# A second chunk's second product by Strassen, with the sums of w_out made one chunk earlier

## The chip, the cores and the metric

The kernel runs on one core of a Trainium2 chip. The metric is the device time of one execution in microseconds. TensorE (PE) multiplies matrices, VectorE (DVE) and ScalarE (ACT) work element by element, GpSimd (POOL) casts values and issues transfers, and SyncE (SP) issues transfers. Each engine takes its own instructions in order; semaphores tie them together.

## The reference

```python
# attention: 8 batches, 8 heads, 576 positions, head size 64
scores = q @ k.T / 8
# heads 0-3: a causal window of 32; heads 4-7: a causal window of 128, every 4th position
attn   = softmax(where(mask, scores, -1e9)) @ v
x      = attn with heads side by side      # 4608 tokens x 512
# feed-forward
h   = x @ w_in                             # 512 x 2048
g   = relu(h) ** 2
out = g @ w_out                            # 2048 x 512, float32
```

## The kernel before

The 4608 tokens are cut into nine chunks of 512 for the feed-forward part; attention runs over eight batches of 576 tokens. Products are in fp16 with sums in float32.

**First product** (`mm1_gen`). For each of 16 slices of 128 hidden features (`ffc`), four matmuls of 512 columns fill one PSUM bank `ph`; ScalarE writes relu into `rt` (L328), VectorE squares it into `g` (L329). A slice is two steps of a generator.

**Second product.** There are three forms. Chunk 0 goes by `mm2_by_rows_gen`, which takes w_out in the order of its four pieces `wo0` to `wo3` as they are loaded. Chunk 1 goes by `mm2_gen`, 64 matmuls of 512 columns (L450), two to a step, 32 steps; ScalarE copies each bank `po` into `ot` (L471) and SP stores it, four stores of 256 KB. Chunks 2 to 8 go by `mm2_strassen_gen`: the matrix of 512 tokens x 2048 features times 2048 x 512 is cut into quarters, and seven products of half size take the place of eight. Each product is 16 matmuls of 256 columns (L382), four to a step, 28 steps in all; the results are gathered in three banks `pa`, `pb` and `pc`. This form needs sums of the quarters of g and of w_out:

- of g, per chunk: `sum_of_g` (L338, L339), called after slices 11 and 15, two instructions each; the difference at L413 before the first product; the difference at L425 after the fourth. They read and write `gs0`, `gs1` and `g`.
- of w_out, once: `sums_of_w_out`, eight differences (L355) into `wt0` to `wt3`. They are handed out one at a time, after each even slice of chunk 1's first product.
- the results: three ScalarE copies (L398) and three VectorE additions (L409), two stores of 512 KB.

**Order.** The order is written out by hand. Attention is emitted piece by piece, and after each piece `pump(n)` emits n steps of the pending feed-forward generator, so TensorE has matmuls while ScalarE takes exponentials and VectorE multiplies by masks (`AT`, L572 and L573) and divides (`rcp`, `xs`, `xd`, L614 and L619). Chunk 0's second product is mixed with batch 1's attention, chunk 1 with batch 2's, chunk 2 with batch 3's. For batch 2 the pump is called with 22, then four times 4, then ten times 2. Attention's PSUM tiles (`ps`, `pz`, `pav`, `paw`) take turns in two double banks.

**Transfers around it.** Batch 3's q and k of the sliding heads are loaded by POOL into `ns`, reordered by VectorE into `nr` (L120), written by SP to device memory as `dp` (L224) and read back by a transposing transfer into `QKTp` (L232), which batch 3's first scores `ps` (L582) read. `turn_and_load` emits this chain, with the loads of the next v (`sv`, `sd`) between the write and the transposes; for batch 2 it is called after the third `av_sliding`. The dilated heads go from device memory to device memory (`dd`, POOL, L214) and by transposes into `QKTd` (L236). w_out's pieces are loaded by POOL (L153): pieces 0 and 1, then batch 1's q and k, then piece 2, and piece 3 later. SP's queue is in order, so stores that stand behind transposes wait for their issue.

## Time and profile before

| | |
|---|---|
| median of 8 executions | 306.73 us (304.44 to 309.36) |
| the profiled execution | 309.36 us, span 307.4 us |
| TensorE busy | 288.0 us, 94% |
| VectorE busy | 212.2 us, 69% |
| ScalarE busy | 173.3 us, 56% |
| POOL busy | 63.5 us, 21% |
| matmuls of 512 columns, second product (L450) | 128, 33.1 us busy |
| sums of w_out (L355) | 8, at 66.4 to 79.5 us |

The profile is one execution, here the slowest of the eight; its span runs from the first to the last instruction, and about 2 us of the time lie outside it. Times inside it are counted from the span's start. A busy matmul overlaps the next one, so TensorE's rate is read from the distance of starts or from the chain, not from the mean of one.

### The profile page before, as it was taken

What the parts mean: (1) busy time and instruction counts of PE and PEld (TensorE: products, weight loads), DVE (VectorE), ACT (ScalarE), POOL (GpSimd) and SP (SyncE); (2) the same over time, 40 slices, a digit from 0 to 9 for tenths busy, and PEclk for the clock granted to TensorE, in tenths of its full rate; (3) what the DMA queues carried; (4) which work ended last, traced back from release to release, by engine and by line L of the source; (5) the groups of instructions that cost most, each with busy time, mean ns of one, the idle gap of its engine ahead of it and who ended that gap; (6) DMA issues with size and microseconds to landing.
All of it is one profiled execution on the core that took longest, in us unless ns stands there. A gap on an engine that the chain in (4) does not pass through costs nothing.

```text
span 307.4 us, 6893 instructions
## 1 busy us (share of the span) xinstructions
PE 288.0 (94%) x2762; PEld 193.3 (63%) x2762; DVE 212.2 (69%) x437; ACT 173.3 (56%) x293; POOL 63.5 (21%) x112
## 2 busy tenths in 40 slices
PE   0978999899999899999999999999999999999994
PEld 0635554455555458855898988557855875785583
DVE  7685447858961589579947994899489934834652
ACT  1764647677844683386439633964396346425620
POOL 4292007201340630530026102700230000000000
PEclk9999999999999999999999999999999999999998
DMA  7699996999969999996799989998992230003004
GB/s 110 139 179 215 206 208 95 177 220 232 146 120 226 227 203 205 175 262 121 147 140 276 182 151 178 282 174 172 158 263 25 44 115 34 2 1 139 0 1 136
DMA packets 77471, 46.77 MB, mean 152 GB/s; under 512 B 58432, under 2 KB 69184, under 8 KB 77440
## 3 DMA queue, kind: packets, MB, share of 16 engines
q1 hardware_dynamic: 68688, 32.71, 50.1%
q0 software_dynamic: 8752, 13.63, 26.5%
q8 instruction: 21, 0.34, 0.5%
q14 instruction: 10, 0.08, 0.1%
HBM read 36.70 MB, written 16.52 MB: 173 GB/s over the span
## 4 chain that ended last, share of the span: by engine, by line
PE 72%; DVE 13%; DMA 7%; ACT 3%; issue 2%; POOL 1%; SPq 0%; DVEq 0%; POOLq 0%
PE ph L305 30%; PE pa L382 14%; PE po L450 8%; PE pb L382 7%; DVE AT L573 4%; DMA QKTp<-dp 4%; PE pc L382 3%; DVE g L329 3%; DMA vd<-vd 2%; PE paw L647 2%; DMA ns<-in_q_dram 2%; PE ps L582 2%; DVE xd L619 2%; PE pf L516 1%; ACT AT L572 1%
## 5 line engine op out<-in xcount | busy, mean ns | idle before, releaser
L305 PE MATMUL ph<-xT,wi 128*128 128x512 f16 (+1 forms) x640 | 134.2, 359 | 0.7 <-ACT xT L684 0.7
L328 ACT ACTIVATE rt<-ph 128x512 f16<-128x512 f32 x144 | 86.3, 609 | 44.6 <-PE ph L305 41.5
L305 PEld LDWEIGHTS <-wi 128*128 128x128 f16 x640 | 68.2, 114 | 45.9 <-issue 0.6
L329 DVE TENSOR_TENSOR g<-rt 128x512 f16<-128x512 f16 x144 | 62.5, 445 | 38.5 <-ACT rt L328 37.4
L382 PEld LDWEIGHTS <-g 128*128 128x128 f16 x448 | 43.3, 98 | 6.2
L382 PEld LDWEIGHTS <-gs 128*128 128x128 f16 x336 | 32.0, 98 | 5.3 <-DVE gs L339 1.7
L450 PE MATMUL po<-wo,g 128*128 128x512 f16 x128 | 33.1, 379 | 0.0
L409 DVE TENSOR_TENSOR ov<-pb,ov 128x512 f32<-128x512 f32 x14 | 9.7, 692 | 27.3 <-PE pb L382 13.9
L382 PE MATMUL pa<-wt,gs 128*128 128x256 f16 x224 | 27.6, 273 | 0.8 <-DVE gs L339 0.8
L382 PE MATMUL pb<-wt,g 128*128 128x256 f16 x224 | 27.1, 273 | 0.0
L169 POOL CAST vp<-sv 128x512 f16<-128x512 f32 x24 | 15.1, 660 | 57.3 <-DMA sv<-in_v_dram 57.3
L398 ACT COPY ov<-pa 128x512 f32<-128x512 f32 x14 | 8.2, 587 | 31.8 <-PE pa L382 31.8
L177 POOL CAST vd<-sd 128x512 f16<-128x512 f32 (+1 forms) x32 | 21.8, 707 | 10.8 <-DMA sd<-in_v_dram 10.2
L619 DVE TENSOR_TENSOR xd<-paw,rcp_d 80x512 f16<-80x512 f32 (+1 forms) x32 | 21.9, 684 | 1.1
L573 DVE TENSOR_TENSOR AT<-AT,maskd 128x576 f16<-128x576 f16 x32 | 20.2, 667 | 1.3 <-ACT AT L572 0.4
L572 ACT ACTIVATE AT<-ps 128x576 f16<-128x576 f32 x32 | 19.2, 658 | 2.7 <-PE ps L582 2.3
L572 ACT ACTIVATE AT<-pz 128x576 f16<-128x576 f32 x32 | 19.7, 694 | 1.4 <-PE pz L601 1.2
L573 DVE TENSOR_TENSOR AT<-AT,maskp 128x576 f16<-128x576 f16 x32 | 15.5, 493 | 6.4 <-ACT AT L572 4.8
L619 DVE TENSOR_TENSOR xs<-pav,rcp_p 96x512 f16<-96x512 f32 x24 | 16.5, 686 | 0.8
L398 ACT COPY ou<-pa 128x512 f32<-128x512 f32 x14 | 8.2, 587 | 15.0 <-PE pa L382 15.0
L450 PEld LDWEIGHTS <-g 128*128 128x128 f16 x128 | 10.4, 97 | 8.3
L647 PEld LDWEIGHTS <-AT 128*128 128x128 f16 x256 | 12.0, 98 | 5.6 <-PE paw L647 1.3
(81 smaller groups left out, 278.1 us busy)
## 6 DMA issues: line engine op xcount, KB each, us to landing
sv<-in_v_dram SPq DMA_DIRECT2D x14, 288.0 KB, 5.4
dp<-nr SPq DMA_DIRECT2D x12, 288.0 KB, 3.9
out_dram<-ou SPq DMA_DIRECT2D x6, 512.0 KB, 4.1
out_dram<-ov SPq DMA_DIRECT2D x6, 512.0 KB, 4.4
sd<-in_v_dram SPq DMA_DIRECT2D x8, 320.0 KB, 5.7
ns<-in_k_dram POOLq DMA_DIRECT2D x8, 288.0 KB, 6.9
ns<-in_q_dram POOLq DMA_DIRECT2D x8, 288.0 KB, 7.9
sd<-in_v_dram SPq DMA_DIRECT2D x8, 256.0 KB, 5.5
```

Of the source, the lines that this page charges most:

```text
L169: nc.gpsimd.tensor_copy(vp[b % 2][:, m : m + 2, :, 0:D], sv[:, :, m : m + 2, :].rearrange("p h m d -> p m h d"))
L177: nc.gpsimd.tensor_copy(vd[b % 2][p0:P, t, c : c + 2, :, 0:D], sd[p0:P, t, :, D * c : D * (c + 2)].rearrange("p h (c d) -> p c h d", d=D),)
L305: nc.tensor.matmul(ph[:, t0:t1], wi4[ffc // 4][:, dmk, :, ffc % 4], xT[:, dmk, x0 : x0 + t1 - t0], start=(dmk == 0 and t0 == 0), stop=(dmk ...
L328: nc.scalar.activation(rt, ph[:], ACTF.Relu)
L329: nc.vector.tensor_mul(g[:, ffc, :], rt, rt)
L382: nc.tensor.matmul(banks[bank][:, t], a(k, t), b(k), start=(new and t == 0 and k == 0), stop=(k == HF - 1), skip_group_check=True,)
L398: nc.scalar.copy(ot, banks[A])
L450: nc.tensor.matmul(po, g[:, ffc, t * P : (t + 1) * P], wo[ffc // 4][:, ffc % 4, :], start=(ffc == 0), stop=(ffc == NFF - 1),)
L572: nc.scalar.activation(AT[:, u, 0:UW], ps[:, :, 0 : UW // 2], ACTF.Exp, scale=scale)
L573: nc.vector.tensor_mul(AT[:, u, 0:UW], AT[:, u, 0:UW], mask)
L619: nc.vector.tensor_tensor(out=x, in0=pv, in1=rb, op=ALU.mult)
L647: nc.tensor.matmul(pav[:, e, h * (D + 2) : h * (D + 2) + D + 1], AT[:, 4 + h, off : off + P], vd[b % 2][:, t, 2 * a + e, h, 0 : D + 1], st ...
```

## The change

Chunk 1 also uses `mm2_strassen_gen`, so `mm2_gen` and its stores go. `mm1_gen` no longer hands out w_out's sums, and calls `sum_of_g` for chunk 1. The eight sums of w_out are emitted in another order, first the four that read pieces 0 and 2, then the four that read pieces 1 and 3. The first four are emitted one by one after each of the four transposing steps of batch 1's q and k, the other four together after batch 1's `attn_values`.

```diff
@@ mm1_gen
             nc.vector.tensor_mul(g[:, ffc, :], rt, rt)
-            if c == 1 and ffc % 2 == 0:
-                next(w_sums)
             if sums and ffc % 4 == 3 and ffc >= HF:
                 sum_of_g(g, ffc - 3, ffc + 1)
@@ sums_of_w_out
-        def w(r, c):
-            return [wo[2 * r + n][:, :, HM * c : HM * (c + 1)] for n in range(2)]
-
-        def t(k):
-            return [wt[k][:, 4 * n : 4 * (n + 1)] for n in range(2)]
-
-        for k, x, y in (
-            (0, w(0, 1), w(0, 0)),
-            (1, w(1, 1), t(0)),
-            (2, w(1, 1), w(0, 1)),
-            (3, w(1, 0), t(1)),
-        ):
-            for o, a, b in zip(t(k), x, y):
+        def w(r, c, n):
+            return wo[2 * r + n][:, :, HM * c : HM * (c + 1)]
+
+        for n in range(2):
+            t = [wt[k][:, 4 * n : 4 * (n + 1)] for k in range(4)]
+            for o, a, b in (
+                (t[0], w(0, 1, n), w(0, 0, n)),
+                (t[1], w(1, 1, n), t[0]),
+                (t[2], w(1, 1, n), w(0, 1, n)),
+                (t[3], w(1, 0, n), t[1]),
+            ):
                 nc.vector.tensor_sub(o, a, b)
                 yield
 
     w_sums = sums_of_w_out()
+
+    def sum_w_out(n):
+        for _ in range(n):
+            next(w_sums)
@@ store
-        if c:
-            nc.sync.dma_start(out=out[(c * 4 + t) * P : (c * 4 + t + 1) * P, :], in_=ot)
-        elif t % 2:
+        if t % 2:
             first_out.append((t - 1, halves[c]))
             if t == 1:
                 leave_first()
-
-    def mm2_gen(c, g):
...
@@ moe_gen
         g = hidden(c)
-        yield from mm1_gen(c, g, c > 1)
-        yield from (mm2_strassen_gen if c > 1 else mm2_gen)(c, g)
+        yield from mm1_gen(c, g, True)
+        yield from mm2_strassen_gen(c, g)
@@ batch 1's attention
     for hp in range(2):
         t_sliding(1, n, hp, True)
         pump(3)
+        sum_w_out(1)
     for a in range(2):
         t_dilated(1, m, a, True)
         pump(2)
+        sum_w_out(1)
     attn_scores(1, 2, 1)
     dp = []
     attn_values(1, 1, True, lambda: dp.append(keep_sliding_qk(2, by_token(2, ns))))
+    sum_w_out(4)
     pump(1000)
```

## Prediction

> **What bounds the kernel now.** I read the page first (busy shares), then the chain of work that ended last, then VectorE's timeline and the waits around the stretch that the change touches.

> ```profile
> PE 288.0 (94%) x2762; PEld 193.3 (63%) x2762; DVE 212.2 (69%) x437; ACT 173.3 (56%) x293; POOL 63.5 (21%) x112
> ...
> PE 72%; DVE 13%; DMA 7%; ACT 3%; issue 2%; POOL 1%; SPq 0%; DVEq 0%; POOLq 0%
> ```

> TensorE is the bound over the whole span, but 13% of the chain is VectorE and 7% DMA, so what a saved matmul is worth depends on where it sits. The chain at its undisturbed end gives the price of both forms of the second product:

> ```profile
> 251.30 13.81 PE ph L305 x64
> 265.12 1.75 PE pa L382 x16
> 266.86 0.87 PE pc L382 x8
> ```

> 64 matmuls of 512 columns take 13.81 us (216 ns each); 16 of 256 columns take 1.75 us (109 ns each). Next, the chain where chunk 1 ends and batch 3's attention begins:

> ```profile
> 94.68 2.69 PE po L450 x12
> 97.37 0.88 PE ph L305 x4
> ...
> 98.62 5.36 DMA QKTp<-dp
> ...
> 104.02 0.43 PE ps L582 x12
> ```

> Chunk 1's last 12 matmuls run to 97.37, chunk 2's first 24 to 102.55, and then TensorE stands until 104.02 for batch 3's transposed q and k:

> ```profile
> PE ps L582 <- DMA QKTp<-dp: 1.5, 1, 1.5
> ```

> So whatever chunk 1 saves is handed to a TensorE that already waits 1.5 us for a transfer. What starts that transfer is VectorE's copy `nr`:

> ```profile
> 79.49 1.10 DVE L355 TENSOR_TENSOR wt<-wo,wt 128x1024 f16<-128x1024 f16 x1
> 80.51 1.64 DVE L573 TENSOR_TENSOR AT<-AT,maskd 128x576 f16<-128x576 f16 x2
> 82.07 0.41 DVE L329 TENSOR_TENSOR g<-rt 128x512 f16<-128x512 f16 x1
> 82.41 0.81 DVE L573 TENSOR_TENSOR AT<-AT,maskd 128x576 f16<-128x576 f16 x2
> 83.19 0.20 DVE L614 RECIPROCAL rcp_p<-pav 96x8 f32<-96x8 f32 x1
> 83.42 0.69 DVE L619 TENSOR_TENSOR xs<-pav,rcp_p 96x512 f16<-96x512 f32 x1
> ...
> 86.50 0.80 DVE L120 COPY nr<-ns 128x2304 f16<-128x2304 f16 x1
> ```

> From 75.07 to 84.1 VectorE has no gap; `nr` is queued at the end of that run. After it come, on SP's queue, the writes of `dp` (87.33), the loads of v, and the transposes (95.68).

> **The change part by part.** *TensorE.* 64 x 216 ns = 13.8 us go, 7 products x 16 x 109 ns = 12.2 us come: -1.6 us. Weight loads (98 ns) still fit under a 109 ns matmul. [...] The trace has 216 and 109 ns for just such pairs, so I take -1.6.

> *Steps.* The second product has 28 steps of 0.44 us instead of 32 of 0.43. `pump` hands out 22+16+20 = 58 of them up to the end of batch 2's attention, of which 32 are the first product. So the attention is mixed with the same TensorE work as before, step for step, and the saving appears only at the tail: 2 steps are left instead of 6. Hence `nr`'s place among TensorE's work does not move earlier.

> *w_out's sums leave chunk 1.* Eight sums leave; five of them sat at 66 to 73 us between squares with VectorE idle about 0.36 us each time for ScalarE, and TensorE ran without a gap: worth 0. The three at 75.07, 77.28 and 79.49 (0.69, 0.69, 1.10) are in the gapless run. An instruction starts about 0.08 before its forerunner's end (66.09 + 0.42, next at 66.43), so they free 2.5 - 0.24 = 2.2 us.

> *Strassen's own sums arrive there.* Four sums of g (0.69 each, L338 and L339) and the difference of g (1.22, L413) come before `nr`: 4.0 - 0.4 = 3.6 us. Net +1.4 us. VectorE's waits for TensorE ahead of `nr` (0.19 and 0.42) are used up: +0.8. Then the second pair of mask multiplies moves from 82.41 to beyond 84.27, beside POOL's four casts; the pair beside casts took 1.64, the pair alone 0.81, so up to +0.8 more. `nr` is later by 0.8 to 1.6; I take 1.2. [...] Applied to all five added sums at this trace's ratio (1.10 / 0.69) it would be 2.4 us more, `nr` 3.2 to 4 late; but by the trace POOL rests from 81.8 to 84.3, where most of them fall, so I charge only the mask pair.

> Behind `nr` come the last difference (1.21, L425) and two additions (0.69 each, L409), 2.6 us, against 2.3 us of VectorE waits before (0.59, 1.31, 0.19, 0.20): no catching up. TensorE's third `pav` must wait for the first one's normalise to free its buffer, 0.4 to 1.2 us later than before (85.19), and the last `py` for the last `xd`, which ended at 93.27 and now ends about 94.8 to 95.7. After it come 0.3 of `py` and 2 steps (0.87): chunk 1 ends at 96.0 to 96.9 instead of 97.37. Of 1.6 us some 0.5 to 1.4 survive, 0.8 in the middle; TensorE reaches batch 3's `ps` near 101.8.

> *The transfer.* `nr` 1.2 late means `dp` written 1.2 late. In this execution its two writes landed 7.1 and 6.2 us after issue; for batches 2 and 4 the trace has 3.3 to 4.4. POOL's copies of `dd`, issued at 86.62 and 87.41 just ahead, are the likely cause (my inference). If `dd` sets the landing, a later issue costs 0; if the time from issue is fixed, the full 1.2. I take +0.3 where `dp` is slow as here: q and k arrive at 104.3. Where `dp` lands in 3.9, the arrival is some 3 us earlier: about 101 before (hidden under 102.55), about 102.0 after.

> *w_out's sums arrive in chunk 0.* Four are put behind the copies of batch 1's q and k. VectorE there: copies at 42.87, 44.68, 46.35, 47.83, the first mask multiply at 49.86 after 1.21 idle. The sums (0.69) fit at 43.6, 45.4, 47.1 and 48.6; the fourth lies beside POOL's casts from 48.36 and may take 1.10, ending 49.7. They wait for w_out's pieces 0 and 2; piece 2 is issued at 24.83 and landed 20.3 us later, 45.1, just ahead of the 45.4 at which it is wanted. Queued behind that wait are the copies of QKTd, for which batch 1's dilated scores wait; the 1.21 idle ahead of 49.86 absorbs a piece up to about 1 us late. The other four sums sit behind the last `xd` (62.02), where VectorE idles 3.39 us until 66.09; four take 2.5 us, and piece 3 (50.0 + 4.9) is there. Cost 0; without that cover 0.6 per sum, so I bound the part by 0 and +0.7.

> *Stores.* Four of 256 KB become two of 512 KB, 1.0 MB either way. SP loses the one at 84.66, ahead of `dp`'s, and issues two instead of three after the transposes (104.68). 256 KB more then run ahead of batch 3's halo copies, which land near 109 to 111.6 and are wanted from 112.8 on: 0, at worst +0.3. ScalarE copies four tiles either way.

> **The sum.** The execution profiled took 309.36 us (span 307.4), 2.6 over the median of 306.73. Against itself: TensorE's 0.8 us is lost in the wait, and the gate moves +0.3, so +0.3 from 104 on; behind it TensorE follows without slack, so the shift stays. Where `dp` is not slow: 102.55 before, the later of 101.8 and 102.0 after, about -0.5. Between the two, -0.1: **306.6 us**.

> **Rivals.** *A: nothing measurable (0.54).* As summed, 305.3 to 308.1; for it speak the wait at 104 and VectorE's gapless run. *B: TensorE's saving comes through (0.17).* If VectorE's backlog is smaller and `dp` no longer meets `dd`, all 1.6 us come, and part of the wait may vanish: 305.1, down to 304.5. Against it: the pump gives attention no less TensorE work, so `nr` does not come sooner. *C: the transposes become the gate for good (0.25).* `nr` is 1.6 late and `dp` takes its 6.6 us from there, in executions that had no wait before: the gate goes from 102.55 to about 105.3, +2.7, 309.4; with an only partly slow `dp` 308.4. It decides once `nr` starts after about 88: from there each us late is a us lost. *D: the change stalls chunk 0 (0.04).* Piece 2 of w_out lands 2 us or more late, VectorE stands in front of the copies of q and k, +1 to +2: 308.5.

> A measurement of this kernel can tell about 0.5% (1.5 us) from no change. B gives 0.17 faster, A most of 0.54 same, C and D 0.29 slower. The range, 304.7 to 309.0, takes in A whole, most of B and the lower half of C.

> **What would show it.** Right: 112 matmuls at L382 for chunk 1 in 12.2 us of TensorE; `nr` for batch 3 at 87.3 to 88.1; the third `pav` waiting for a normalise; the wait of `ps` on QKTp grown from 1.5 to 2 to 3 us; sums L355 between 43 and 66 with no wait of TensorE on VectorE there. Wrong: `nr` still at 86.5 or earlier with `ps` near 102 (B); QKTp landing beyond 105.5 (C); a gap on VectorE before L355 around 45 (D).

## The result, and the profile after

| | before | changed |
|---|---|---|
| median | 306.13 us (304.44 to 309.36, 32 executions) | 309.91 us (307.94 to 312.69, 11 executions) |
| ratio | | 1.0117 [1.0089, 1.0145] |
| TensorE busy | 288.0 us | 285.9 us |
| VectorE busy | 212.2 us | 219.1 us |

The kernel became 1.2% slower, outside the range and on the side to which the forecast had given 0.29. The ratio leaves out one slow execution of the changed kernel, the one of 312.69 us. The execution profiled first was the slowest of the kernel before (309.36 us) and the fastest of the changed one (307.94), so setting those two pages side by side would hide the loss. A second profile of each stands nearer its median: 305.3 us (span 303.5) before, 309.41 us (span 307.6) changed. They are called *before, second* and *changed, second*.

The page of the changed kernel, first profile:

```profile
PE 285.9 (93%) x2810; PEld 196.5 (64%) x2810; DVE 219.1 (72%) x446; ACT 173.1 (57%) x293; POOL 66.4 (22%) x112
...
PE 69%; DVE 13%; DMA 9%; ACT 3%; issue 2%; POOL 2%; SPq 0%; DVEq 0%; POOLq 0%
```

TensorE does 2.1 us less and VectorE 6.9 us more than on the page before; the DMA share of the chain rose from 7% to 9%. The busy shares already say that TensorE's part of the bargain was kept. To find where the time went I cut both programs at the first scores of each batch:

| stretch | before, second | changed, second |
|---|---|---|
| chunk 0's first `ph` to batch 2's scores | 49.43 us | 49.74 |
| to batch 3's scores (chunk 1 is in here) | 28.63 | 31.32 |
| to batch 4's | 27.75 | 27.75 |
| to batch 5's | 30.27 | 29.79 |
| to batch 6's | 30.49 | 31.38 |
| to batch 7's | 30.28 | 30.46 |
| to the end | 84.70 | 84.82 |
| sum | 281.55 | 285.26 |

Of +3.71 us, +2.69 arise where chunk 1 is, and +0.89 between batch 5's and 6's scores. Chunk 0 takes a little longer or shorter in every execution, so times "after batch 2's scores" below are counted from the first of these matmuls in the same execution (73.99 us in the first profile of before, 71.41 in its second; 71.03 and 72.08 in those of the changed kernel).

VectorE ahead of `nr`, changed kernel, first profile:

```profile
78.86 0.41 DVE L329 TENSOR_TENSOR g<-rt 128x512 f16<-128x512 f16 x1
79.31 0.69 DVE L336 TENSOR_TENSOR gs<-g 128x1024 f16<-128x1024 f16 x1
80.03 0.69 DVE L337 TENSOR_TENSOR gs<-gs,g 128x1024 f16<-128x1024 f16 x1
80.64 1.63 DVE L413 TENSOR_TENSOR g<-g 128x2048 f16<-128x2048 f16 x1
82.19 1.64 DVE L561 TENSOR_TENSOR AT<-AT,maskd 128x576 f16<-128x576 f16 x2
83.76 0.19 DVE L602 RECIPROCAL rcp_p<-pav 96x8 f32<-96x8 f32 x1
83.98 0.69 DVE L607 TENSOR_TENSOR xs<-pav,rcp_p 96x512 f16<-96x512 f32 x1
...
86.26 0.75 DVE L120 COPY nr<-ns 128x2304 f16<-128x2304 f16 x1
```

and what TensorE waits for in the same execution (us in total, times, longest):

```profile
PE pav L619 <- DVE rcp_p L602: 2.3, 1, 2.3
...
PE ps L570 <- DMA QKTp<-dp: 1.2, 1, 1.2
```

The normalise (`rcp_p`, `xs`) that frees a `pav` buffer is queued behind `L336`, `L337`, `L413` and two mask multiplies, and TensorE's third `pav` stands 2.3 us for it. The reader should see two prices here: `L413` took 1.63 us, where the forecast had 1.22, and the mask pair 1.64, where a pair alone takes 0.81. `nr` starts 15.23 us after batch 2's scores and the third `pav` 13.79, in both profiles of the changed kernel; in both of before it was 12.5 and 11.2. `nr` is 2.7 late and the third `pav` 2.6.

POOL at that moment, first the changed kernel's first profile, then before, second:

```profile
80.05 4.26 POOL L177 CAST vd<-sd 128x512 f16<-128x512 f32 x4 [1.79 <-DMA sd<-in_v_dram]
```

```profile
80.67 2.40 POOL L177 CAST vd<-sd 128x512 f16<-128x512 f32 x4 [1.98 <-DMA sd<-in_v_dram]
```

The four casts of v take 4.26 us beside VectorE's sums and 2.40 without `L413` beside them, and `dd`'s copies follow the casts on POOL (the first is issued at 84.26 and at 83.01).

Then the clock. The changed kernel, second profile, by stretches (length, PE, PEld, DVE, ACT and POOL busy, granted TensorE clock, DMA share, GB/s):

```profile
82.81:86.22 3.41, 1.11 (x16) 0.81 (x15) 3.34 (x7) 1.20 (x2) 3.35 (x5) 1.00 0.00 0
86.22:89.63 3.41, 3.41 (x23) 2.58 (x20) 2.94 (x5) 1.15 (x2) 0.19 (x1) 0.50 0.89 138
```

and its chain over the same time:

```profile
85.87 0.42 PE pav L619 x8
86.28 1.64 PE pb L382 x8
87.92 0.48 PE px L648 x6
88.40 1.54 PE pb L382 x8
```

In the first row TensorE is busy 1.11 of 3.41 us, because of the wait. Then the granted clock is at half for 3.41 us, from 86.2 on. Eight matmuls of 256 columns take 1.64 and 1.54 us instead of 0.87: about 1.7 us lost while TensorE shows as fully busy. In the first profile of the changed kernel the clock stayed at 1.0 after the same wait, and it paid at the next gate instead, batch 3's transposed q and k. Its chain, and that of before, second:

```profile
95.46 6.45 DMA QKTp<-dp
...
101.95 0.43 PE ps L570 x12
```

```profile
94.92 5.08 DMA QKTp<-dp
...
100.04 0.43 PE ps L582 x12
```

So the ledger of that stretch, against before, second, is -1.6 (TensorE's work), +2.3 (wait at the third `pav`), and then either +1.7 (half clock; second profile, with +0.3 not assigned: +2.7) or +1.2 (`ps` waiting for QKTp; first profile, +0.4 not assigned: +2.3). The two ends are nearly the same gate. In the second profile QKTp landed at 103.22, 31.1 us after batch 2's scores, and TensorE came to `ps` only 0.18 us later; in the first it landed after 30.9 us, before after 30.0 and 28.6. With a full clock, TensorE in the second profile would have come earlier and, if the transfer landed when it did, would have waited for it. So the 1.7 us are no net price: that stretch is only 0.4 us longer than in the first profile.

The +0.89 us farther on are a wait too. In the second profile of the changed kernel batch 6's scores wait for their transposed q and k (waits from 170 to 193 us); in that of before they do not:

```profile
PE ps L570 <- DMA QKTp<-dp: 0.8, 1, 0.8
```

### The profile page after: what moved, and what is told of

The parts are those of the page before. It is cut to its first block, busy times and chain, and to the rows that moved or that the text cites. A ratio compares the mean times of both kernels' runs of the same rounds, so it can differ in the third digit from the quotient of the medians.

```text
span 306.0 us, 6995 instructions
## 1 busy us (share of the span) xinstructions
PE 285.9 (93%) x2810; PEld 196.5 (64%) x2810; DVE 219.1 (72%) x446; ACT 173.1 (57%) x293; POOL 66.4 (22%) x112
## 4 chain that ended last, share of the span: by engine, by line
PE 69%; DVE 13%; DMA 9%; ACT 3%; issue 2%; POOL 2%; SPq 0%; DVEq 0%; POOLq 0%
PE ph L305 29%; PE pa L382 15%; PE pb L382 8%; PE po L450 4%; DMA QKTp<-dp 4%; DMA vd<-vd 4%; PE pc L382 3%; DVE g L329 3%; PE paw L635 2%; DVE AT L561 2%; DVE gs L336 2%; DVE xd L607 2%; ACT AT L560 2%; PE ps L570 1%; DMA sv<-in_v_dram 1%
## 5 line engine op out<-in xcount | busy, mean ns | idle before, releaser
L305 PE MATMUL ph<-xT,wi 128*128 128x512 f16 (+1 forms) x640 | 134.2, 359 | 0.7 <-ACT xT L672 0.7
L305 PEld LDWEIGHTS <-wi 128*128 128x128 f16 x640 | 68.2, 114 | 45.6 <-issue 0.6
L329 DVE TENSOR_TENSOR g<-rt 128x512 f16<-128x512 f16 x144 | 63.2, 451 | 32.5 <-ACT rt L328 31.3
L382 PEld LDWEIGHTS <-g 128*128 128x128 f16 x512 | 49.1, 98 | 7.4 <-DVE g L329 0.4
L382 PEld LDWEIGHTS <-gs 128*128 128x128 f16 x384 | 36.3, 98 | 6.1 <-DVE gs L337 2.1
L382 PE MATMUL pa<-wt,gs 128*128 128x256 f16 x256 | 31.9, 273 | 1.0 <-DVE gs L337 1.0
L409 DVE TENSOR_TENSOR ov<-pb,ov 128x512 f32<-128x512 f32 x16 | 11.1, 692 | 28.5 <-ACT ov L398 14.2
L382 PE MATMUL pb<-wt,g 128*128 128x256 f16 x256 | 31.2, 273 | 0.0
L169 POOL CAST vp<-sv 128x512 f16<-128x512 f32 x24 | 15.5, 680 | 53.2 <-DMA sv<-in_v_dram 27.6
L177 POOL CAST vd<-sd 128x512 f16<-128x512 f32 (+1 forms) x32 | 24.1, 781 | 9.9 <-DMA sd<-in_v_dram 9.0
L561 DVE TENSOR_TENSOR AT<-AT,maskd 128x576 f16<-128x576 f16 x32 | 18.6, 604 | 2.2 <-ACT AT L560 0.9
L450 PE MATMUL po<-wo,g 128*128 128x512 f16 x64 | 17.1, 380 | 0.0
L382 PE MATMUL pc<-wo,g 128*128 128x256 f16 x128 | 16.9, 273 | 0.0
L382 PE MATMUL pa<-wo,g 128*128 128x256 f16 x128 | 16.3, 273 | 0.0
## 6 DMA issues: line engine op xcount, KB each, us to landing
sv<-in_v_dram SPq DMA_DIRECT2D x14, 288.0 KB, 5.7
dp<-nr SPq DMA_DIRECT2D x12, 288.0 KB, 4.0
ns<-in_k_dram POOLq DMA_DIRECT2D x8, 288.0 KB, 6.1
ns<-in_q_dram POOLq DMA_DIRECT2D x8, 288.0 KB, 7.5
```

Source lines behind the costliest of these rows:

```text
L169: nc.gpsimd.tensor_copy(vp[b % 2][:, m : m + 2, :, 0:D], sv[:, :, m : m + 2, :].rearrange("p h m d -> p m h d"))
L177: nc.gpsimd.tensor_copy(vd[b % 2][p0:P, t, c : c + 2, :, 0:D], sd[p0:P, t, :, D * c : D * (c + 2)].rearrange("p h (c d) -> p c h d", d=D),)
L305: nc.tensor.matmul(ph[:, t0:t1], wi4[ffc // 4][:, dmk, :, ffc % 4], xT[:, dmk, x0 : x0 + t1 - t0], start=(dmk == 0 and t0 == 0), stop=(dmk ...
L329: nc.vector.tensor_mul(g[:, ffc, :], rt, rt)
L382: nc.tensor.matmul(banks[bank][:, t], a(k, t), b(k), start=(new and t == 0 and k == 0), stop=(k == HF - 1), skip_group_check=True,)
L409: nc.vector.tensor_add(ot, banks[bank], ot)
```

## The experiments

My theory after the result: what Strassen's sums add to VectorE ahead of a normalise makes TensorE wait, and POOL's casts beside VectorE and the clock enlarge it. The rivals: the moved sums of w_out do harm; the transposing transfers are the gate and VectorE has little to do with it; the saving of TensorE is itself not there.

**Only the sums of w_out moved.** Chunk 1 keeps its direct product.

```diff
 # against before: the change's sums_of_w_out, sum_w_out and its calls, and
-            if c == 1 and ffc % 2 == 0:
-                next(w_sums)
```

> The sums of w_out move into chunk 0 as in the change, but chunk 1 keeps its direct second product. Theory G (VectorE's added sums make the copy nr for batch 3 late, and the transposes of batch 3 become the gate): VectorE has less to do ahead of nr than before, so nr is up to 1.5 us earlier and the time is at most that of before, 305 to 306.5 us. Theory S (the moved sums cost chunk 0 time, by waits for w_out's pieces or by contention with POOL): most of the 3.8 us shows, 309 or more.

Measured: 306.21 us, ratio 1.0002 [0.9975, 1.0030]. The move costs nothing, and taking three sums off VectorE's dense run brings nothing. The one risk that the forecast named is visible in the trace, the wait of a sum for w_out's piece 2:

```profile
43.05 0.69 DVE L351 TENSOR_TENSOR wt<-wo,wt 128x1024 f16<-128x1024 f16 x1 [0.66 <-DMA wo<-in_moe_w_out_dram]
```

0.66 us, and the slack behind it takes it. `nr` stays where it was, 12.5 us after batch 2's scores. All the harm is in the Strassen part.

**VectorE's load alone.** To the last kernel, VectorE's sums of Strassen's sizes are added in Strassen's places, with results that nothing reads; TensorE still does the direct product.

```diff
-        yield from mm1_gen(c, g, c > 1)
+        yield from mm1_gen(c, g, True)
@@ mm2_gen
+        nc.vector.tensor_sub(gs[0], g[:, 0:HF, 0:HTOK], g[:, 0:HF, HTOK:])
...
+                if t == 1 and ffc == 11:
+                    nc.vector.tensor_sub(gs[1], g[:, HF:, 0:HTOK], g[:, HF:, HTOK:])
```

> As the run with the moved sums alone, and VectorE also gets sums of the same size at the same places as Strassen's (four of 1024, two of 2048 elements, their results are not used), while TensorE keeps the direct product. Theory G: VectorE's load is the cause, so nr is 2 us or more late and the time rises to 308.5 to 311, with no gain of TensorE to set against it. Theory T (the cause is in the Strassen form itself on TensorE and ScalarE or in its two large stores at the end): stays at 305 to 307.

Measured: 309.66 us, 1.0114 [1.0051, 1.0177], as slow as the change, without one Strassen matmul in chunk 1. TensorE's wait is there too:

```profile
PE pav L634 <- DVE rcp_p L617: 2.7, 1, 2.7
```

In its trace the third `pav` comes 13.79 us after batch 2's scores and `nr` 15.24, as in the change (13.79 and 15.23), and batch 3's scores after 31.08. This is the run that settles the main cause: the load on VectorE, in that place, is enough.

**Strassen without its sums of g in chunk 1.** The counterpart: TensorE's saving with VectorE's load taken away.

```diff
         def sq(n):
+            if c == 1:
+                return gq(1, 1)
...
+        if c > 1:
             nc.vector.tensor_sub(g[:, 0:HF, HTOK:], g[:, 0:HF, 0:HTOK], g[:, 0:HF, HTOK:])
...
-        yield from mm1_gen(c, g, True)
+        yield from mm1_gen(c, g, c > 1)
```

> The change, but chunk 1's sums of g are left out on VectorE (the products read quarters of g in their place): the same matmuls, copies, additions and stores. Theory G: nr comes as early as before or earlier, chunk 1 keeps TensorE's 1.6 us, 304 to 306. Theory T: still 308.5 to 311.

Measured: 307.81 us, 1.0050 [1.0027, 1.0072]: 2.1 us below the change, but not below before. The kernel leaves out the sums of g in chunk 1; its products read quarters of g in their place. The `pav` wait is gone, `nr` is back at 12.44, and TensorE reaches batch 3's scores 27.1 us after batch 2's instead of 28.6 with the moved sums alone (28.87 less a wait of 0.31 for QKTp): 1.5 of the 1.6 us are seen. They run into the transfer:

```profile
PE ps L574 <- DMA QKTp<-dp: 2.5, 1, 2.5
```

and then into the clock (stretches as above):

```profile
100.00:102.00 2.00, 0.01 (x2) 0.10 (x3) 0.43 (x1) 0.13 (x1) 1.94 (x4) 0.99 1.16 246
102.00:104.00 2.00, 2.00 (x16) 1.02 (x16) 0.79 (x2) 1.19 (x2) 0.86 (x2) 0.50 1.10 240
```

So there is a second barrier behind the first: QKTp, as the forecast's likeliest case had it, but with half a clock in its wake.

**Is it `nr` or `dd` that sets QKTp?** First `nr` earlier: `turn_and_load` for batch 2 is called from the fourth scores, as for batch 3.

```diff
-        attn_scores(b, 4, 0, {3: turn_and_load} if b == 3 else {})
-        attn_values(b, b, False, turn_and_load)
+        attn_scores(b, 4, 0, {3: turn_and_load})
+        attn_values(b, b, False)
```

> The change, with batch 3's copy nr and the transfers behind it emitted after batch 2's last scores, ahead of its values (as the kernel does for batch 4). Theory G: nr starts about 2.5 us earlier than in the change and the gate goes with it: 306 to 308. Theory P (the loss is TensorE's own waiting in chunk 1 for VectorE, nr only a bystander): no gain, 309 to 311, since VectorE's work in front of the pav tiles grows by 0.75.

Measured: 309.88 us, 1.0111 [1.0053, 1.0170]. The new place lies in VectorE's backlog as well: `nr` came 13.1 us after batch 2's scores, 2.1 sooner than in the change, but now stood ahead of the normalises:

```profile
PE pav L619 <- DVE rcp_p L602: 3.1, 1, 3.1
```

Both kernels were then profiled once more, which gave the second profiles used above.

> The kernel before, a second profile, since the first one was its slowest execution of eight. If theory D holds (the gate on batch 3's first scores sits about 17.5 us after POOL issues the copies dd, whoever is slow), the gate minus that issue is 17 to 18 us here too, and TensorE waits less than 1 us or not at all.

> The changed kernel, a second profile, since the first was its fastest of eleven and 2 us under its median. Expected: the third pav waits 2 to 3 us for VectorE, and the wait on batch 3's q and k is longer than 1.2 us, or the TensorE clock is halved for one stretch of about 3.4 us after it, as in the run without the sums of g.

Measured: 305.3 us and 309.41 us, one execution each. In before, QKTp landed 17.0 us after the first `dd`, with almost no wait; the change has the wait at `pav` and the half clock behind it, as expected.

Next `dd` earlier: POOL issues its copies between the casts of the sliding and the dilated v, in the change and in before.

```diff
-            cast_v(b)
+            cast_sliding_v(b)
         dd = keep_dilated_qk(nxt)
+        if b == 2:
+            cast_dilated_v(b)
```

> The change, with POOL issuing batch 3's dd between the casts of batch 2's sliding and dilated v instead of after both, about 4 us earlier. Theory D (dd starts the backlog of transfers that ends in the gate): q and k of batch 3 arrive 2 to 4 us earlier, no wait on them and no halved clock; what stays is TensorE's wait for VectorE at the third pav, so 307 to 308.5. Theory G (nr alone sets the gate): no gain, 309 to 311.

> The kernel before with the same earlier dd. Theory D: its executions lose up to 1 us of waiting, 305 to 306.2. If dd then collides with the loads of v that batch 2 waits for, 306.5 to 308.

Measured: 309.06 us, 1.0107 [1.0055, 1.0159] on the change; 305.62 us, 0.9983 [0.9957, 1.0009] on before. Although `dd` was issued about 6 us sooner, batch 3's scores of the change started 30.93 us after batch 2's, as in the change's first profile (30.92). My idea that the gate stands a fixed 17.5 us behind `dd`'s issue, whatever else happens, falls: here the distance was 23.7.

Both together, `dd` early and the sums of g in chunk 1 left out:

> The change without chunk 1's sums of g (left out), and dd issued earlier. Without the sums TensorE came to batch 3's first scores 1.6 us earlier and then waited 2.5 us for the transposes and ran at half clock for 3.4 us. Theory D: the transposes now come in time, no half clock: 303.5 to 305, faster than before. If the gate hangs on the later transfers alone: 307 to 308.

Measured: 306.68 us, 1.0014 [0.9990, 1.0038].

```profile
PE ps L574 <- DMA QKTp<-dp: 0.9, 1, 0.9
```

Batch 3's scores come 28.00 us after batch 2's. `dd` early alone left them at 30.93, `nr` early alone (no sums of g) brought 29.59; only both bring the 3 us. The 18 traces fit one reading, a gate at the later of two chains: in the ten with `dd` as written QKTp lands 16.9 to 18.0 us after the first `dd` is issued, and in the eight with `dd` early 14.2 to 15.5 us after `nr` starts. With these distances the two chains of the change end within about a microsecond of each other (`nr` at 15.2 and `dd` at 13.2 us after batch 2's scores), so moving one shows little. Yet even with these barriers lowered the kernel only returns to the time of before: between batch 5's and 6's scores it takes 31.83 us (before, second: 30.49), 1.4 of them a wait for QKTp, and to batch 7's 31.02 (30.28).

**Moving the large difference.** `L413`'s difference is emitted only in the third product, two steps in; then with `dd` early as well; then with two more feed-forward steps ahead of batch 2's attention.

```diff
-        nc.vector.tensor_sub(g[:, 0:HF, HTOK:], g[:, 0:HF, 0:HTOK], g[:, 0:HF, HTOK:])
+        if c > 1:
+            difference()
...
-        yield from product(A, sq(1), tq(1))
+        for n, _ in enumerate(product(A, sq(1), tq(1))):
+            if c == 1 and n == 1:
+                difference()
+            yield
```

> The change, with the difference of g (1.6 us on VectorE, L413) emitted two steps into the third product, so behind the first pav's normalise instead of ahead of batch 2's last mask multiplies. Theory P (TensorE's 2.3 us wait at the third pav, and the half clock after it, are the loss): that wait falls to about 0.8, a second one of about 1 appears at the first product that reads the difference, no clock is halved: 307.5 to 308.7. Theory D (the gate by transfers is the loss): no change, 309.5 to 310.5.

> As the run with the late difference, and dd issued by POOL between the casts of sliding and dilated v. Theory P with D as a second barrier: 306 to 307.5. P alone: as the run without the earlier dd.

```diff
-        pump(22 if b == 2 else 12)
+        pump(24 if b == 2 else 12)
```

> As the run with late difference and early dd, and 24 instead of 22 steps of chunk 1 ahead of batch 2's attention: the first two sums of g (1.4 us) fall where VectorE waits for ScalarE anyway, ahead of the dense stretch. If VectorE's queue ahead of the pav tiles is the cause, the wait at the third pav is gone: 305 to 306.5. If not, as the run with 22.

Measured: 309.93 us, 1.0144 [1.0107, 1.0181]; 309.37 us, 1.0123 [1.0095, 1.0151]; 310.02 us, 1.0134 [1.0093, 1.0175]. No gain. The waits of the first of these:

```profile
PE ps L577 <- DMA QKTp<-dp: 2.3, 1, 2.3
...
PE pav L626 <- ACT ov L398: 0.8, 1, 0.8
PE pb L382 <- DVE g L412: 0.6, 1, 0.6
```

The wait at `pav` is only split in two, one part now at the product that reads the difference, and what TensorE gains meets QKTp at once; behind that wait the clock is at half for 3.41 us, from 103.4 on (mean clock 0.993). In the third, the wait for `g` (L412) is 1.7 us.

**Work for TensorE in the wait.** Eight matmuls of 512 columns that nothing reads go ahead of batch 2's third `av_sliding`, so that TensorE does not stand.

```diff
         for mp in range(3):
+            if b == 2 and mp == 2:
+                keep_clock(8)
             av_sliding(b, mp, xs)
```

> The change, with eight matmuls of 512 columns (1.7 us, result unused) ahead of the third pav of batch 2, where TensorE waits 2.3 us for VectorE. Theory H (the wait lets the TensorE clock fall to half for 3.4 us in many executions, at 1.7 us each): the half clock there is gone, and the median falls from 309.9 to about 308.7 although TensorE does more. If the clock is not part of it: 309.9 or more.

Measured: 308.82 us, 1.0081 [1.0052, 1.0109]: with some 1.7 us more work for TensorE (8 x 216 ns), not slower than the change; the two intervals overlap. The clock after the wait stays up:

```profile
86.00:88.00 2.00, 2.00 (x30) 1.84 (x29) 1.97 (x5) 0.96 (x2) 0.00 (x0) 1.00 1.04 175
```

The mean granted clock was 0.994 or less in 1 of its 10 executions, in 8 of the 12 of the changed kernel whose clock is on record, and in 9 of 98 of before. Within the changed kernel those eight have a median of 310.76 us; three of the other four lie at 307.94 to 308.71. One stretch of 3.41 us at half speed makes a mean of 0.994, but the mean does not say where it lay: of the five profiled executions with such a stretch it follows a wait at `pav` or QKTp in three, and in two (the versions without casts and with two more steps) it lies at 25 to 30 us, in chunk 0. That the half clock behind the wait makes the eight slower is therefore likely, not shown.

The same with `dd` early:

> Filler and earlier dd together. Theory H with D: neither half clock, about 308. If only the number of VectorE's instructions counts, as the change with the earlier dd, 309.

Measured: 309.46 us, 1.0126 [1.0082, 1.0170]; 2 of 4 executions have the lower clock. Here the filler did not help.

**POOL's casts.** As the change with `dd` early, with POOL's four casts of the dilated v of batch 2 left out.

```diff
         dd = keep_dilated_qk(nxt)
-        if b == 2:
-            cast_dilated_v(b)
```

> As the change with the earlier dd, but POOL's four casts of batch 2's dilated v are left out. If VectorE's lateness comes from running beside them: the difference of g takes 1.2 instead of 1.6 us, the mask pair 0.8 instead of 1.6, the wait at the third pav falls from 2.3 to about 1.1, and the time to 307 to 308. If from the number of instructions: the wait stays at 2 or more, 308.5 to 309.5.

Measured: 308.11 us, 1.0071 [1.0040, 1.0101], between the change with `dd` early (1.0107) and before. VectorE's timeline and TensorE's wait:

```profile
82.29 1.22 DVE L413 TENSOR_TENSOR g<-g 128x2048 f16<-128x2048 f16 x1
83.42 0.82 DVE L561 TENSOR_TENSOR AT<-AT,maskd 128x576 f16<-128x576 f16 x2
```

```profile
PE pav L619 <- DVE rcp_p L602: 1.1, 1, 1.1
```

1.63 has become 1.22, 1.64 has become 0.82, and the wait 1.1 us, within the forecast's 0.4 to 1.2. The third `pav` comes 12.55 us after batch 2's scores and `nr` 13.99: 1.3 and 1.5 later than before, where the change had 2.6 and 2.7. What was missing in the forecast is what these casts add to `L413` and the mask pair, 1.24 us. In the medians the gain, about 1 us, is not clear of the noise: the intervals of the runs with and without casts overlap.

**What is left worth having.** The moved sums with `dd` early, without Strassen in chunk 1:

> Chunk 1's second product direct as before, w_out's sums moved into chunk 0, dd issued earlier. VectorE has 2.2 us less ahead of nr than before and the transposes 4 us more room: 304.8 to 305.8, the fastest here. If TensorE alone bounds that stretch, as before, 306.

Measured: 305.82 us, 0.9999 [0.9983, 1.0015]. No version here is measurably faster than before.

## Why the prediction was wrong

*TensorE -1.6 us: right.* 16 matmuls of 256 columns took 1.75 us in the changed kernel as in before, and without the sums of g TensorE came 1.5 us sooner. The trace's own 216 and 109 ns were the right price.

*The sums of w_out in chunk 0 cost 0: right,* 1.0002 [0.9975, 1.0030], with a wait of 0.66 us for piece 2 that the slack absorbed.

*The attention gets no less TensorE work, so `nr` gains nothing: right.* Neither `nr` nor the tail of attention came sooner.

***`nr` 0.8 to 1.6 late, third `pav` 0.4 to 1.2 late: this is the step that failed.*** Measured from batch 2's scores, `nr` is 2.7 late and the third `pav` 2.6. The counting of instructions was sound (VectorE's run "without a gap" has two of 0.11 us, too small to matter); the price of them was not: without the casts beside them `nr` is 1.5 late and the third `pav` 1.3, nearly as forecast, and what the casts add makes up the other 1.24 us. The forecast took 0.4 us of overlap and 1.22 for `L413`, and charged the casts only to the mask pair, because POOL rested from 81.8 to 84.3 in the profile of before. That gap was POOL waiting 2.43 us for `sd`, a transfer. POOL's casts began 10.3 us after batch 2's scores in that profile, but 9.0 to 9.3 after them in the three others, and `L413`, at 9.6, fell beside them. Measured with and without casts beside them, `L413` takes 1.63 and 1.22 us and the mask pair 1.64 and 0.82; the four casts take 4.26 and 2.40 with and without `L413` beside them. The forecast did weigh the slowing for all five added sums, at 2.4 us more and `nr` 3.2 to 4 late; the truth, 2.7, lies between. The ratio used there (1.10 / 0.69) was not sound either: here the addition is about 0.41 us for an instruction (last section), 2.1 us for five by my estimate. I set the slowing aside on the strength of an idle gap whose end was the landing of a transfer, and that landing came 1.0 us sooner in the second profile of before than in the first.

*The clock: not in the forecast at all.* The forecast reckoned a TensorE wait at its length. In one of the two profiles of the change 3.41 us of half speed follow it, and 8 of the 12 executions measured along with the other have a mean clock as low. It is an addition, not the cause: `dd` early on the change and `turn_and_load` early on it had no execution at the lower clock in four each, and stood at 309.06 and 309.88 us.

*Batch 3's transfer: there, but too small in the sum.* The `ps` wait on QKTp did exist and did take what TensorE saved, as the likeliest case had it. That it depends on `nr` and on `dd`, whichever ends later, was left undecided there ("if `dd` sets the landing, a later issue costs 0"). `dp` did land sooner, in 3.6 to 4.6 us instead of 5.8 to 7.1. Still QKTp landed 30.9 and 31.1 us after batch 2's scores, against 30.0 and 28.6 before: +0.9 between the first profiles, where the forecast had +0.3, and +2.5 between the second, where it had +1.0. That the casts, slower beside VectorE's sums (4.26 against 2.40 us), also put off POOL's issue of `dd` (13.2 us after batch 2's scores, against 12.6 and 11.6) stood nowhere in it.

*"Of 1.6 us some 0.5 to 1.4 survive": none did.* After batch 2's scores, chunk 1's last matmul ends at 24.6 and 26.2 us in the change, at 23.4 in both profiles of before: 1.2 later, and 2.8 with the half clock, instead of 0.5 to 1.4 sooner.

*Rival C* named the sign and nearly the size (+2.7, 309.4), and much of the road: in the times of the first profile it had `nr` start after about 88 and QKTp land at about 105.3, which is 31.3 us after batch 2's scores; the change has 30.9 and 31.1. It was wrong in that `dp` would take 6.6 us, and it did not have TensorE's wait at `pav`, which with the half clock behind it fills the time up to the same gate. Which of the two barriers would cost how much without the other is not settled: VectorE's load raises both, and each version that lowered only one, with the sums in place, met the other.

*Open.* All kernels that are Strassen in chunk 1 need 30.9 to 31.8 us between batch 5's and 6's scores, the six profiles with a direct chunk 1 30.5 to 30.9. The difference is a wait: in all twelve profiles of the former, batch 6's scores stand 0.3 to 1.4 us for QKTp, in the six of the latter not at all. The second transpose lands 5.5 to 6.6 us after its issue in the twelve, 4.3 to 4.6 in the six. In the version with the other barriers lowered this wait (1.4 us) is more than that version gains at batch 3's scores (28.00 against 28.63 us). It does not come from VectorE's load (the version with that load alone has none of it); why the transfer takes longer was not tried.

## What to carry to other kernels

An engine that is not the bound may still have a stretch without a gap; work added there is paid by whoever waits at its end (here 2.3 us at the third `pav`). Price the added instructions as the trace shows them beside a busy neighbour (here `L413` at 1.63 us beside POOL's casts, not 1.22), unless the idle gap that speaks against it is held by something that cannot move. A saving on the bounding engine is worth having only where the next wait behind it is already farther away than the saving is long.

## What the runs showed of the hardware that was not expected

```profile
79.56:82.97 3.41, 2.95 (x36) 2.17 (x34) 3.38 (x4) 2.01 (x5) 2.86 (x3) 1.00 0.02 4
82.97:86.38 3.41, 1.56 (x24) 1.49 (x25) 3.31 (x9) 0.79 (x2) 2.40 (x4) 1.00 0.24 22
```

In the second profile the whole wait falls into one beat and TensorE is busy 1.11 us of it; in the first the wait is split over two beats and the emptier one still has 1.56 us. The two first profiles end the same way: their last beats before the half clock have 1.15 us of TensorE work (before, 302.23 to 305.65) and 0.38 (changed, 301.42 to 304.83), and all their other beats since the first change 1.56 us or more, without half clock behind them. So in these three traces a wait was dear or cheap by where it fell in the beat, which no change of the kernel here controls; a beat a third busy (1.11 of 3.41 us) was enough. Two stretches of half clock in chunk 0 (in the versions without casts and with two more steps, mean clock 0.992 and 0.994) follow beats with 2.1 us of busy time, much of it in small matmuls; they don't fit this reading and stay open. A busy TensorE hides the loss: only the granted clock, or the price of eight equal matmuls (0.87 against 1.64 us), shows it.

VectorE's instructions and POOL's casts beside each other cost both: four casts of 128x512 go from 2.40 to 4.26 us, 0.60 to 1.07 each, and VectorE's instructions on fp16 tiles gain up to about 0.41 us each around this stretch, whatever their length: a square of 512 elements 0.42 to 0.83, one mask multiply of 576 0.45 to 0.86, a sum of 1024 0.69 to 1.10, the difference of 2048 1.22 to 1.63. Elsewhere two mask multiplies beside casts took more, 1.51 us (at 164.7, changed, first profile) and 2.04 (at 17.2, before, first profile). The normalises, which read `pav`, stay at 0.69 beside the same casts; why these do and the others don't, no run shows. So short instructions suffer more in proportion, and a ratio taken from one of them misleads.
